# Decoding weights with an integer addition, and the last score tile of a head in one pass

## The chip, the cores and the metric

The kernel runs on one core of one Trainium2 chip. The metric is the device time of one execution in microseconds (us), lower is better. TensorE (PE) runs matmuls and loads its stationary operand (PEld), VectorE (DVE), ScalarE (ACT) and GpSimd (POOL) work elementwise, and SyncE (SP) issues most DMAs. Each engine takes its instructions in the program's order.

## The reference

Attention with a threshold over 4 batches of 8 heads (576 positions, head width 64), then two feed-forward blocks on 2304 tokens of width 512:

```python
scores = scale * np.matmul(q, k.transpose(0, 1, 3, 2))
thresh = np.max(scores, axis=-1, keepdims=True) - tau
scores = np.where(scores >= thresh, scores, -1000000000.0)
attn = exp(scores - max); attn = attn / (sum + 1e-09); x = attn @ v
...
h = x @ w_in                                     # 512 -> 2048
g = np.where(h >= 1, h, np.where(h <= -1, 0.0, (h + 1) ** 2 / 4)); y = g @ w_out
...
h = y @ w_in2; solu = h * softmax(h)             # 512 -> 1024
out = (layernorm(solu) * g_ln) @ w_out2
```

The four weight matrices come as 64-bit floats (the launch hands them over as 64-bit integers); the kernel turns them into 32-bit floats on the chip.

## The kernel before

**Precision.** A 32-bit product is made of matmuls on fp32r tiles: an operand is split into a rounded part (hi) and a rest (lo), and three products are summed.

**Attention** comes first (about 0 to 361 us). The 32 heads go in 16 pairs, a pair in 9 units: 4 units for the even head, one for the rests of 64 keys of both heads, 4 for the odd head. Each unit makes scores turned around (tile zt, keys on partitions), subtracts the row's threshold within the matmuls, and then: ACT takes the exponential (e, L416), DVE masks it (L421), ACT rounds it (phi, L429), POOL makes the rest (plo, L430), and three units later (LAGV) PE multiplies with the values (av, `values`, L453).

Ahead of that a head needs its row maxima: five score tiles (`scores`, L319) of 128 queries, the last with 64 queries and 64 empty rows, each of two passes of two matmuls with 288 columns. Stacked operands make a pass: q_st holds lo of q in its upper 64 rows and hi in its lower ones, k_st hi above and lo below, so pass one sums the two mixed products; q_m and k_on give hi times hi in pass two. `row_max` (L335) reduces a tile from PSUM on DVE; `row_shift` follows on ACT and POOL. Scores of a pair are made in units -10 to -2 relative to its own first one (S_UNITS), so the even head's tiles begin in the ninth unit of the second pair before it and end in the fourth unit of the pair before, and the odd head's begin in the fifth unit of that pair, two there.

**Stacking.** A head's q and k are transposed on PE (tr, L271), split on ACT and DVE (q_st L279, lo L280), and moved into place by DMAs that SP issues: `stack_k` (k_both<-q_st, k_both<-lo, q_m<-q_st, L289 to L291) and two units later `stack_q` (q_st<-lo, L295), which must wait until k_both<-q_st has landed, since it overwrites what that one reads. On the same queue stand the stores of finished heads (sums<-xs, x<-xs, L467 and L468, behind ACT's copy xs<-av, L465), loads of later pairs, and the weight loads raw (L542, 512 KB each).

**Buffers.** Score tiles, zt tiles and transposes take turns in three PSUM buffers (ps_r); a tile can start when the reader of the third one before it is through.

**Order.** Within a unit a string of letters (ORDER) sets the order: E zt and exponential, S a score tile, x its maximum, M the mask, p phi and plo, v and V values, J a step of the decode jobs, F, P, A, T, L the rest. A job is a Python generator; after each yield it waits so many steps, and in some units (DECODE) only certain kinds of step are let in: kind "b" in attention only in a pair's fourth unit. In attention 8 blocks of weights (128 by 512) are decoded one after the other, a new one at least 14 units after the last and at most two under way; 40 more follow later, up to three under way and a new one every third step.

**Decoding** (`words_to_f32`, L506): on the 32-bit halves of the numbers, ACT takes the absolute value of the upper half, DVE clamps, shifts and combines (L514, L517, L520), cuts out the power of two (L524) and scales the lower half with it (L527), POOL adds it (L531); ACT and POOL then split into hi and lo (L558, L560).

**First feed-forward block** (to about 757 us): per 128 columns of h, 12 matmuls (L793), then DVE, ACT, DVE, ACT and POOL make g (cl, gh, gl, L811 to L816), then 12 matmuls for y (L833). **Second block** to the end (L877, L988).

Of the kernel before, what the change touches and what calls it, by code (L numbers as in the profile page):

```python
# [21 lines left out]
def kernel(  # L22
# [16 lines left out]
    P = 128  # L39
# [26 lines left out]
    KEEP = {-8: 1, -7: 1, -6: 1, -5: 1, -4: 1, -3: 4, -1: 6, 0: 4, 1: 4, 2: 4}  # L66
    TURN_AT = 4
    JOB_EVERY = 14

# [90 lines left out]
    q_m = bufs4([R3, SP], F32R, "q_m")  # L160
    NV = 10
    v_nat = [early_p.tile([P, NV, D], F32, name=f"v_nat{i}") for i in range(2)]
    v_hi = [att_p.tile([P, NV, P], F32R, name=f"v_hi{i}") for i in range(2)]
    v_lo = [att_p.tile([P, NV, D], F32R, name=f"v_lo{i}") for i in range(2)]
# [16 lines left out]
    def setup_fill(i, eng):  # L181

        for j in range(2):
# [15 lines left out]
    def setup_ones():  # L199
        for t in v_hi:  # L200
            nc.gpsimd.memset(f32(t[:, 0:8, D:P]), 1.0)
            for half in range(2):
                for n in range(2):
                    nc.gpsimd.memset(f32(t[64 * half : 64 * half + 64, 8 + n, D:P]), float(n == half))

# [79 lines left out]
    def stack_k(h):  # L285
# [4 lines left out]
        nc.sync.dma_start(f32(k_st[j][i][D:P, o]), f32(tr_t[h][0:D, :]))  # L290
        nc.sync.dma_start(f32(q_m[j][i][0:D, 0:S]), f32(q_st[j][i][D:P, 0:S]))  # L291

    def stack_q(h):
# [22 lines left out]
    sc_ps = {}  # L316
    mcol = {}

    def scores(h, n):  # L319
        j, i = buf(h)  # L320
        o = key_off(h)
        ps = ps_r.tile([P, 2, 512], F32, tag="r", name="sc")
        for st, kk in ((q_st, k_st), (q_m, k_on)):
            r = slice(0, P if st is q_st else R1)
            for c in range(2):
# [4 lines left out]
                    start=(st is q_st),  # L330
                    stop=(st is q_m),
                )
        sc_ps[h, n] = ps

    def row_max(h, n):  # L335
        if n == 0:
            mcol[h] = att_p.tile([P, NTI], F32, tag="mcol", name="mcol", bufs=2)
        mc = mcol[h]
# [96 lines left out]
    def values(u, j):  # L435
# [14 lines left out]
        vh, vl = v_hi[p % 2][:, vn, :], v_lo[p % 2][:, vn, :]  # L450
        for o, vv, pp in ((P, vh, hi), (D, vl, hi), (P, vh, lo)):
            for c in range(2):
                nc.tensor.matmul(  # L453
                    ps[0:o, c, 0:HS], lhsT=vv, rhs=pp[:, c, :],
                    start=first and pp is hi and o == P, stop=last and pp is lo,
                )
            yield

    def store_head(h):
# [3 lines left out]
        else:  # L463
            xs = raw_p.tile([P, 1024], F32, tag="raw", name="xs")[:, 0:S].rearrange("p (c s) -> p c s", c=2)
        nc.scalar.copy(xs, av_ps.pop(h)[:, :, 0:HS])  # L465
        r = slice(D * (hh % 2), D * (hh % 2) + D)
# [39 lines left out]
    def words_to_f32(raw, n, got):  # L506

        upper, lower = raw[:, :, 1], raw[:, :, 0]
        a = wt_p.tile([P, 512], F32, tag="w", name="dec_a")[:, 0:n]
        au, cu = a.bitcast(U32), upper  # L510
        c = cu.bitcast(F32)
        nc.scalar.activation(out=a, in_=upper.bitcast(F32), func=ACTF.Abs)
        yield 1, "s"
        nc.vector.tensor_scalar(a, a, MAG_LOW, MAG_HIGH, op0=ALU.max, op1=ALU.min)  # L514
        if fine[0]:
            yield 1, "s"
        nc.vector.tensor_scalar(au, au, 3, 0x3FFFFFF8, op0=ALU.logical_shift_left, op1=ALU.bitwise_and)  # L517
        if fine[0]:
            yield 1, "b"
        nc.vector.scalar_tensor_tensor(  # L520
            out=au, in0=upper, scalar=0xC0000000, in1=au, op0=ALU.bitwise_and, op1=ALU.bitwise_or
        )
        yield 1, "s"
# [181 lines left out]
    for p in range(NP):  # L705
        s_units = S_FIRST[p] if p < 2 else S_UNITS
        for n, d in enumerate(s_units):
            at(s_at, UNITS * p + d, None, 2 * p + n // NTI, n % NTI)
        for j in range(2):
# [9 lines left out]
    def attention_unit(u):  # L719
# [7 lines left out]
        sc = iter(s_at.get(u, ()))  # L727
        mx = iter(s_at.get(u, ()))
        for what in ORDER[u % UNITS]:
            if what == "E" and 0 <= u < NU:  # L730
# [9 lines left out]
            elif what == "x":  # L740
                for _, a in itertools.islice(mx, 1):
                    row_max(*a)
            elif what == "M" and 0 <= u < NU:
                mask(u)
            elif what == "p" and 0 <= u - 1 < NU:
# [425 lines left out]
```

## Time and profile before

| | us |
|---|---|
| median of 3 runs | 968.86 (968.29 to 971.03) |
| profiled execution | 968.04 |
| its span, first to last instruction | 966.3 |
| PE busy in it | 944.8 |
| DVE, ACT, POOL busy in it | 711.9, 493.9, 603.3 |

The profile is of one execution. Times in it count from the first instruction. A matmul's duration covers its way through the array, and matmuls overlap, so what one costs is the distance between starts. "Idle before" is the time in which the engine had nothing to do ahead of an instruction, and behind the arrow stands what ended it, as far as the trace can tell. The granted clock of PE is full over the whole span (mean 0.999 of 2.4 GHz).

### The profile page before, as it was taken

How to read it: one execution, taken by the hardware profiler on the slowest of the kernel's cores; microseconds unless marked ns; L12 is line 12 of the kernel's file. 1: busy time of each engine (PE TensorE's matmuls, PEld its weight loads, DVE VectorE, ACT ScalarE, POOL GpSimd, SP SyncE). 2: the span in 40 equal slices, each digit the busy share in tenths (PEclk: the TensorE clock that was granted, in tenths of full speed). 3: DMA queues.
4: the chain of work that ended last, by engine and by line, in shares of the span. 5: the costliest groups of instructions: out<-in, count | busy, mean ns of one | idle time of the engine just before them, and what ended most of it. 6: DMA issues, size and time to landing. Idle time of an engine off the chain costs nothing.

```text
span 966.3 us, 15184 instructions
## 1 busy us (share of the span) xinstructions
PE 944.8 (98%) x5299; PEld 842.3 (87%) x5299; DVE 711.9 (74%) x1132; ACT 493.9 (51%) x924; POOL 603.3 (62%) x575
## 2 busy tenths in 40 slices
PE   7999999999999989999999999999999999999998
PEld 7899899999989978889888988898889988888886
DVE  5788888788788875898678876888675676666562
ACT  3667677777767675354333433333334444344433
POOL 7678788888978898677445544654547614334422
PEclk9999999999999999999999999999999999999999
DMA  6665666657666314211311131112311124444443
GB/s 144 148 147 124 152 159 145 170 126 176 157 142 154 81 44 98 68 66 44 120 44 66 44 119 45 65 45 77 129 34 45 44 66 131 109 120 124 138 119 90
DMA packets 89726, 99.61 MB, mean 103 GB/s; under 512 B 50000, under 2 KB 62608, under 8 KB 89648
## 3 DMA queue, kind: packets, MB, share of 16 engines
q1 hardware_dynamic: 87952, 97.97, 38.5%
q8 instruction: 42, 0.69, 0.3%
q10 hardware_dynamic: 1696, 0.66, 0.3%
q14 instruction: 36, 0.29, 0.1%
HBM read 55.13 MB, written 15.88 MB: 73 GB/s over the span
## 4 chain that ended last, share of the span: by engine, by line
PE 79%; POOL 8%; issue 4%; DVE 4%; ACT 3%; DMA 1%; ACTq 0%; POOLq 0%; DVEq 0%
PE y L833 18%; PE h L793 18%; PE o L988 10%; PE h L877 10%; PE av L453 9%; PE zt L403 6%; PE sc L326 6%; POOL plo L430 3%; PE tr L271 1%; POOL wg L560 1%; DMA nat<-in_q_dram 1%; DVE mcol L339 1%; POOL dec_a L531 1%; POOL xl L769 1%; ACT phi L429 1%
## 5 line engine op out<-in xcount | busy, mean ns | idle before, releaser
L430 POOL TENSOR_TENSOR plo<-e,phi 128x576 fp32r<-128x576 f32 x144 | 207.6, 1451 | 48.9 <-ACT phi L429 48.8
L816 POOL TENSOR_TENSOR gl<-cl,gh 128x512 fp32r<-128x512 f32 (+1 forms) x80 | 100.3, 1254 | 160.0 <-ACT gh L815 85.3
L793 PE MATMUL h<-xh,wg 128*128 128x512 f32 (+1 forms) x640 | 184.1, 369 | 0.7 <-DVE e L421 0.7
L833 PE MATMUL y<-gh,wg 128*128 128x512 f32 (+1 forms) x640 | 184.6, 369 | 0.0
L421 DVE SCALAR_TENSOR_TENSOR e<-zt,ntau,e 128x576 f32<-128x576 f32 x144 | 117.3, 815 | 54.5 <-ACT e L416 34.8
L793 PEld LDWEIGHTS h<-xh,wg 128*128 128x128 f32 x640 | 118.4, 188 | 16.7 <-DVE e L421 1.0
L833 PEld LDWEIGHTS y<-gh,wg 128*128 128x128 f32 x640 | 118.5, 188 | 15.9
L416 ACT ACTIVATE e<-zt 128x576 f32<-128x576 f32 x144 | 93.9, 652 | 70.0 <-PE zt L403 53.2
L339 DVE TENSOR_REDUCE mcol<-sc 128x1 f32<-128x576 f32 x160 | 116.7, 748 | 4.9 <-PE sc L326 4.7
L833 PE MATMUL y<-gl,wg 128*128 128x512 f32 (+1 forms) x320 | 118.8, 371 | 0.9 <-POOL gl L816 0.9
L793 PE MATMUL h<-xl,wg 128*128 128x512 f32 (+1 forms) x320 | 117.8, 368 | 0.0
L815 ACT CAST gh<-cl 128x512 fp32r<-128x512 f32 (+1 forms) x80 | 46.3, 579 | 111.9 <-DVE cl L814 110.7
L812 ACT ACTIVATE cl<-cl,half 128x512 f32<-128x512 f32 (+1 forms) x80 | 54.4, 679 | 95.4 <-DVE cl L811 95.4
L988 PE MATMUL o<-wg,ln 128*128 128x512 f32 x432 | 102.7, 393 | 0.0
L877 PE MATMUL h<-wg,y 128*128 128x512 f32 x432 | 101.1, 390 | 0.0
L988 PEld LDWEIGHTS o<-wg,ln 128*128 128x128 f32 x432 | 80.9, 188 | 18.8 <-ACT ln L951 0.4
L429 ACT CAST phi<-e 128x576 fp32r<-128x576 f32 x144 | 96.2, 668 | 1.5 <-ACT mt L369 0.7
L952 POOL TENSOR_TENSOR ln<-land,ln 128x1024 fp32r<-128x1024 f32 x16 | 38.5, 2404 | 91.7 <-ACT ln L951 85.0
L877 PEld LDWEIGHTS h<-wg,y 128*128 128x128 f32 x432 | 81.0, 188 | 16.8
L811 DVE TENSOR_SCALAR cl<-h 128x512 f32<-128x512 f32 (+1 forms) x80 | 50.6, 632 | 51.1 <-PE h L793 49.0
L326 PE MATMUL sc<-k_both,q_st 128*128 128x288 f32 x320 | 72.2, 307 | 6.5 <-issue 1.8
L403 PE MATMUL zt<-q_st,k_both 128*128 128x288 f32 x320 | 72.4, 308 | 1.6 <-DVE lo L280 1.3
(114 smaller groups left out, 1883.2 us busy)
## 6 DMA issues: line engine op xcount, KB each, us to landing
raw<-in_moe_w_in_dram SPq DMA_DIRECT2D x24, 512.0 KB
raw<-in_moe_w_out_dram SPq DMA_DIRECT2D x24, 512.0 KB
k_both<-q_st SPq DMA_DIRECT2D x30, 288.0 KB
sq<-so SPq DMA_DIRECT2D x64, 128.0 KB
land<-sq SPq DMA_DIRECT2D x16, 512.0 KB
k_both<-lo SPq DMA_DIRECT2D x32, 144.0 KB
q_st<-lo SPq DMA_DIRECT2D x32, 144.0 KB
x<-xs SPq DMA_DIRECT2D x32, 144.0 KB
```

Of the source, the lines that this page charges most:

```text
L326: nc.tensor.matmul(ps[:, c, 0:HS], lhsT=st[j][i][r, n * P : n * P + P], rhs=kk[j][i][r, o + c * HS : o + (c + 1) * HS], start=(st is q_st) ...
L339: nc.vector.tensor_reduce(mc[:, n : n + 1], sc_ps.pop((h, n))[:, :, 0:HS], axis=AXES.XY, op=ALU.max, negate=True)
L403: nc.tensor.matmul(ps[:, c, 0:HS], lhsT=st, rhs=mv[:, c * HS : (c + 1) * HS], start=(m == 0), stop=(m == len(todo) - 1),)
L416: nc.scalar.activation(out=e, in_=st_ps[u][:, :, 0:HS], func=ACTF.Exp)
L421: nc.vector.scalar_tensor_tensor(out=e, in0=st_ps.pop(u)[:, :, 0:HS], scalar=ntau[:, 0:1], in1=e, op0=ALU.is_ge, op1=ALU.mult)
L429: nc.scalar.copy(hi, e)
L430: (nc.vector if u - NU in LO_DVE or u < NU - UNITS and u % UNITS in LO_UNITS else nc.gpsimd).tensor_tensor(lo, e, f32(hi), op=ALU.subtract)
L793: nc.tensor.matmul(ps, lhsT=a[:, kk, f], rhs=m[:, kk, :], start=(n == 0 and kk == 0), stop=(n == 2 and kk == KD - 1),)
L816: nc.gpsimd.tensor_tensor(gl, cl, f32(gh), op=ALU.subtract)
L833: nc.tensor.matmul(y_ps[c][d], lhsT=a[:, jj, ds_], rhs=m, start=(jj == 0 and n == 0), stop=(jj == JG - 1 and n == 2),)
L877: nc.tensor.matmul(ps[g], lhsT=a[:, kk, :], rhs=wg_t["in2", g][s][:, kk, :], start=(n < 2), stop=(n >= 6 * KD - 2),)
L988: nc.tensor.matmul(ps, lhsT=a[:, f, :], rhs=wg_t["out2", f // 4][m][:, f % 4, :], start=(n == 0), stop=(n == len(terms) - 1))
```

## The change

Three edits.

*Decoding.* The shift keeps no mask, the sign is put in by exclusive or, and the two DVE steps L524 and L527 are gone. ACT instead turns the lower half into a float 2 + lower * 2^-51, whose bit pattern is a constant plus the rounded top bits of the lower half, and POOL adds the two patterns as 32-bit integers. In attention a job has two yields fewer, later one.

*One pass.* For heads from the third pair on, the last score tile takes only pass one: a further DMA (q_st<-q_st) puts hi of the 64 queries into the 64 empty columns, so that the matmul gives the mixed products on partitions 0 to 63 and hi times hi on 64 to 127. ACT copies the second half down (main), DVE adds and reduces in one instruction, which stands behind the mask of the unit. Odd heads make this tile first of five instead of last.

*Narrower.* v_hi carries 2 columns of ones instead of 64, so that the stationary operand of two of three av groups has 66 columns instead of 128, and only 65 partitions of av are copied. The tiles mcol become two fixed ones, zeroed at the start.

```diff
     def stack_k(h):
         ...
         nc.sync.dma_start(f32(q_m[j][i][0:D, 0:S]), f32(q_st[j][i][D:P, 0:S]))
+        if h >= ONE_PASS:
+            nc.sync.dma_start(f32(q_st[j][i][0:D, S:SP]), f32(q_st[j][i][D:P, M4:S]))
...
     def scores(h, n):
-        for st, kk in ((q_st, k_st), (q_m, k_on)):
+        passes = ((q_st, k_st), (q_m, k_on))[0 : 2 if n < NM or h < ONE_PASS else 1]
+        for st, kk in passes:
...
     def row_max(h, n):
+        mc = mcol[h] = mcols[h % 2]
+        if n == NM and h >= ONE_PASS:
+            ps = sc_ps.pop((h, n))
+            t = att_p.tile([64, 2, HS], F32, tag="half", name="main", bufs=1)
+            nc.scalar.copy(t, ps[64:P, :, 0:HS])
+            def finish():
+                nc.vector.tensor_tensor_reduce(
+                    out=t, in0=ps[0:64, :, 0:HS], in1=t, scale=-1.0, scalar=3.0e38,
+                    op0=ALU.add, op1=ALU.min, accum_out=mc[0:64, n : n + 1],
+                )
+            return finish
...
     def values(u, j):
-        for o, vv, pp in ((P, vh, hi), (D, vl, hi), (P, vh, lo)):
+        for o, vv, pp in ((VW, vh, hi), (D, vl, hi), (VW, vh, lo)):
...
     def words_to_f32(raw, n, got):
-        nc.vector.tensor_scalar(au, au, 3, 0x3FFFFFF8, op0=ALU.logical_shift_left, op1=ALU.bitwise_and)
+        nc.vector.tensor_scalar(au, au, 3, None, op0=ALU.logical_shift_left)
+        nc.scalar.activation(out=lower.bitcast(F32), in_=lower, func=ACTF.Copy, bias=2.0, scale=2.0 ** -51)
         if fine[0]:
             yield 1, "b"
         nc.vector.scalar_tensor_tensor(
-            out=au, in0=upper, scalar=0xC0000000, in1=au, op0=ALU.bitwise_and, op1=ALU.bitwise_or
-        )
-        yield 1, "s"
-        nc.vector.tensor_scalar(cu, au, 0xFF800000, None, op0=ALU.bitwise_and)
-        if fine[0]:
-            yield 1, "b"
-        nc.vector.scalar_tensor_tensor(
-            out=c, in0=lower, scalar=2.0 ** -52, in1=c, op0=ALU.mult, op1=ALU.mult
+            out=au, in0=upper, scalar=0x80000000, in1=au, op0=ALU.bitwise_and, op1=ALU.bitwise_xor
         )
         yield 1, ""
-        nc.gpsimd.tensor_tensor(a, a, c, op=ALU.add)
+        nc.gpsimd.tensor_tensor(au, au, lower, op=ALU.add)
...
+            m = n % NTI
+            if p > 1 and n >= NTI:
+                m = (m + NTI - 1) % NTI
```

How it moves instructions, first on PE in the fourth and fifth unit of the ninth pair, before and after (numbers tell buffers: 98 and 103 are of the even head 18, 102 and 107 of the odd head 19, whose scores begin here; `sc` score tile, `zt` turned scores, `av` values):

```order
L403 MATMUL zt<-q_st_105,k_both_100 128x288 x2
L403 MATMUL zt<-q_m_110,k_both_100 128x288 x2
L326 MATMUL sc<-k_both_98,q_st_103 128x288 x2
L326 MATMUL sc<-k_both_98,q_m_108 128x288 x2
L453 MATMUL av<-phi,v_hi_115 128x288 x2
...
L403 MATMUL zt<-q_m_111,k_both_101 128x288 x2
L326 MATMUL sc<-k_both_102,q_st_107 128x288 x2
L326 MATMUL sc<-k_both_102,q_m_112 128x288 x2
L326 MATMUL sc<-k_both_102,q_st_107 128x288 x2
L326 MATMUL sc<-k_both_102,q_m_112 128x288 x2
```

```order
L421 MATMUL zt<-q_st_105,k_both_100 128x288 x2
L421 MATMUL zt<-q_m_110,k_both_100 128x288 x2
L334 MATMUL sc<-k_both_98,q_st_103 128x288 x2
L471 MATMUL av<-phi,v_hi_115 66x288 x2
...
L421 MATMUL zt<-q_m_111,k_both_101 128x288 x2
L334 MATMUL sc<-k_both_102,q_st_107 128x288 x4
L334 MATMUL sc<-k_both_102,q_m_112 128x288 x2
```

The even head's last tile and the odd head's first have lost their second pass; nothing else stands between them than before.

On DVE in the same two units, before and after (`raw` and `dec_a` are of decoding, `mcol` are row maxima, `ISA` is the joint add and reduction with the reading of its accumulator):

```order
L280 SCALAR_TENSOR_TENSOR lo<-tr,scale_119,q_st_104 128x576
L339 TENSOR_REDUCE mcol<-sc 128x1
L421 SCALAR_TENSOR_TENSOR e<-zt,ntau,e 128x576
L527 SCALAR_TENSOR_TENSOR raw<-raw 128x512
L421 SCALAR_TENSOR_TENSOR e<-zt,ntau,e 128x576
L339 TENSOR_REDUCE mcol<-sc 128x1 x2
```

```order
L284 SCALAR_TENSOR_TENSOR lo<-tr,scale_119,q_st_104 128x576
L439 SCALAR_TENSOR_TENSOR e<-zt,ntau,e 128x576
L351 ISA main,mcol_122<-sc,main 64x576
L351 ISA mcol_122 64x1
L439 SCALAR_TENSOR_TENSOR e<-zt,ntau,e 128x576
L351 ISA main,mcol_123<-sc,main 64x576
L351 ISA mcol_123 64x1
L357 TENSOR_REDUCE mcol_123<-sc 128x1
```

The reduction of the even head's last tile moved behind the mask, and the decode step between the two masks is gone here; in 8 of the 14 pairs concerned a decode step stands before the second mask, where before it was all 14.

On SP around a weight load, before ahead of an odd head's stacking, and after within an even head's (`raw` the load, `k_both` and `q_st` the stacking):

```order
L468 DMA x<-xs 64x576
L542 DMA raw<-in_moe_w_out_dram 128x1024
L289 DMA k_both_101<-q_st_106 64x2x576
L290 DMA k_both_101<-lo 64x576
L291 DMA q_m_111<-q_st_106 64x576
```

```order
L293 DMA k_both_100<-q_st_105 64x2x576
L294 DMA k_both_100<-lo 64x576
L295 DMA q_m_110<-q_st_105 64x576
L297 DMA q_st_105<-q_st_105 64x64
L553 DMA raw<-in_moe_w_out_dram 128x1024
L301 DMA q_st_105<-lo 64x576
```

Of the loads in attention that have a head's stacking close behind, five stood ahead of an odd head's k_both; after, two do, two stand between an even head's k_both and its q_st<-lo, and one between an odd head's.

## Rows read from the trace of the kernel before

**Rows 1.** Page, busy time of each engine, share of the span, instructions.

```profile
PE 944.8 (98%) x5299; PEld 842.3 (87%) x5299; DVE 711.9 (74%) x1132; ACT 493.9 (51%) x924; POOL 603.3 (62%) x575
```

**Rows 2.** Windows: stretch, us, busy us of engines (count), clock, DMA.

```profile
100.00:200.00 100.00, 97.29 (x713) 93.44 (x712) 82.18 (x113) 72.40 (x140) 83.29 (x86) 1.00 0.64 154
400.00:450.00 50.00, 49.12 (x240) 42.93 (x240) 44.56 (x57) 23.23 (x42) 37.54 (x29) 1.00 0.24 80
```

**Rows 3.** Timeline, PE: start, us, what, count; three av groups.

```profile
202.35 0.43 PE L453 MATMUL av<-phi,v_hi 128*128 128x288 f32 x2
202.62 0.42 PE L453 MATMUL av<-phi,v_lo 128*64 128x288 f32 x2
202.88 0.43 PE L453 MATMUL av<-plo,v_hi 128*128 128x288 f32 x2
```

**Rows 4.** Page, costliest groups: count, busy us, mean ns, idle before, its end.

```profile
L833 PE MATMUL y<-gl,wg 128*128 128x512 f32 (+1 forms) x320 | 118.8, 371 | 0.9 <-POOL gl L816 0.9
...
L326 PE MATMUL sc<-k_both,q_st 128*128 128x288 f32 x320 | 72.2, 307 | 6.5 <-issue 1.8 <-DVE dec_a L520 1.6 <-DMA q_st<-lo 1.4
```

**Rows 5.** Timeline, SP and PE, to an odd head's first score tile.

```profile
201.66 0.55 SPq L295 DMA_DIRECT2D q_st<-lo  x1
...
203.95 0.43 PE L403 MATMUL zt<-q_m,k_both 67*128 67x288 f32 x2
...
204.21 0.49 PE L326 MATMUL sc<-k_both,q_st 128*128 128x288 f32 x2
```

**Rows 6.** Timeline, PE and SP: the same tile in two other pairs.

```profile
268.55 0.50 PE L326 MATMUL sc<-k_both,q_st 128*128 128x288 f32 x2 [1.64 <-DVE dec_a L520]
...
328.34 0.59 SPq L295 DMA_DIRECT2D q_st<-lo  x1
...
330.88 0.51 PE L326 MATMUL sc<-k_both,q_st 128*128 128x288 f32 x2 [0.52 <-issue]
```

**Rows 7.** Timeline, DVE and PE, fifth unit of the pair of rows 5.

```profile
204.18 1.03 DVE L527 SCALAR_TENSOR_TENSOR raw<-raw 128x512 f32<-128x512 uint32 x1
...
205.16 0.82 DVE L421 SCALAR_TENSOR_TENSOR e<-zt,ntau,e 128x576 f32<-128x576 f32 x1
...
206.13 0.43 PE L403 MATMUL zt<-q_st,k_both 128*128 128x288 f32 x2
```

**Rows 8.** Groups by form, whole span, DVE, ACT and POOL.

```profile
L339 DVE TENSOR_REDUCE mcol<-sc 128x1 f32<-128x576 f32 x160 | 116.7, 748 | 4.9 <-PE sc L326 4.7 <-POOL q_st L190 0.2
...
L527 DVE SCALAR_TENSOR_TENSOR raw<-raw 128x512 f32<-128x512 uint32 x48 | 39.7, 826 | 1.4
...
L524 DVE TENSOR_SCALAR raw<-dec_a 128x512 uint32<-128x512 uint32 x48 | 27.5, 573 | 0.0
...
L905 DVE DVE_READ_ACCUMULATOR so<-h,st,so 128x1 f32 x36 | 3.0, 83 | 0.0
...
L465 ACT COPY xs<-av 128x576 f32<-128x576 f32 x32 | 20.5, 640 | 26.9 <-PE av L453 22.3 <-DMA nat<-in_k_dram 1.5 <-DMA k_both<-lo 1.5
...
L531 POOL TENSOR_TENSOR dec_a<-dec_a,raw 128x512 f32<-128x512 f32 x48 | 67.4, 1403 | 5.1 <-DVE raw L527 5.1
...
L952 POOL TENSOR_TENSOR ln<-land,ln 128x1024 fp32r<-128x1024 f32 x16 | 38.5, 2404 | 91.7 <-ACT ln L951 85.0 <-PE o L988 6.8
```

**Rows 9.** Groups by form, whole span, weight loads of av.

```profile
L453 PEld LDWEIGHTS av<-phi,v_hi 128*128 128x128 f32 x320 | 50.9, 189 | 2.9 <-ACT xs L465 1.7
...
L453 PEld LDWEIGHTS av<-phi,v_lo 128*64 128x64 f32 x320 | 42.3, 135 | 0.0
```

**Rows 10.** Timeline, DVE and PE, a shift at the third unit's end.

```profile
116.21 1.61 DVE L517 TENSOR_SCALAR dec_a<-dec_a 128x512 uint32<-128x512 uint32 x1
...
118.60 0.54 PE L403 MATMUL zt<-q_st,k_both 128*128 128x288 f32 x2 [0.68 <-DVE lo L280]
```

**Rows 11.** Timeline, POOL and PE near the end of attention.

```profile
341.99 1.29 POOL L560 TENSOR_TENSOR wg<-dec_a,wg 128x512 fp32r<-128x512 f32 x1
...
344.71 0.53 PE L453 MATMUL av<-plo,v_hi 128*128 128x288 f32 x2 [0.84 <-POOL plo L430]
```

More of the change, by code (lines that the diff above doesn't have):

```diff
@@ L67 @@
     TURN_AT = 4
+    ONE_PASS = 4
     JOB_EVERY = 14
@@ L161 @@
     NV = 10
+    VW = D + 2
     v_nat = [early_p.tile([P, NV, D], F32, name=f"v_nat{i}") for i in range(2)]
-    v_hi = [att_p.tile([P, NV, P], F32R, name=f"v_hi{i}") for i in range(2)]
+    v_hi = [att_p.tile([P, NV, VW], F32R, name=f"v_hi{i}") for i in range(2)]
     v_lo = [att_p.tile([P, NV, D], F32R, name=f"v_lo{i}") for i in range(2)]
@@ L181, in setup_fill @@
     def setup_fill(i, eng):
+        if i < 2:
+            eng.memset(mcols[i], 0.0)
         for j in range(2):
@@ L200, in setup_ones @@
         for t in v_hi:
-            nc.gpsimd.memset(f32(t[:, 0:8, D:P]), 1.0)
+            nc.gpsimd.memset(f32(t[:, 0:8, D:VW]), 1.0)
             for half in range(2):
                 for n in range(2):
-                    nc.gpsimd.memset(f32(t[64 * half : 64 * half + 64, 8 + n, D:P]), float(n == half))
+                    nc.gpsimd.memset(f32(t[64 * half : 64 * half + 64, 8 + n, D:VW]), float(n == half))
     nat_t = {}
@@ L317 @@
     mcol = {}
+    mcols = [att_p.tile([P, NTI], F32, name=f"mcol{i}") for i in range(2)]
     def scores(h, n):
@@ L330, in scores @@
                     start=(st is q_st),
-                    stop=(st is q_m),
+                    stop=(st is passes[-1][0]),
                 )
@@ L335, in row_max @@
     def row_max(h, n):
-        if n == 0:
-            mcol[h] = att_p.tile([P, NTI], F32, tag="mcol", name="mcol", bufs=2)
-        mc = mcol[h]
+        mc = mcol[h] = mcols[h % 2]
[9 more added lines that the diff above has]
+            return finish
         nc.vector.tensor_reduce(
@@ L454, in values @@
                     ps[0:o, c, 0:HS], lhsT=vv, rhs=pp[:, c, :],
-                    start=first and pp is hi and o == P, stop=last and pp is lo,
+                    start=first and pp is hi and o == VW, stop=last and pp is lo,
                 )
@@ L464, in store_head @@
             xs = raw_p.tile([P, 1024], F32, tag="raw", name="xs")[:, 0:S].rearrange("p (c s) -> p c s", c=2)
-        nc.scalar.copy(xs, av_ps.pop(h)[:, :, 0:HS])
+        nc.scalar.copy(xs[0:R1], av_ps.pop(h)[0:R1, :, 0:HS])
         r = slice(D * (hh % 2), D * (hh % 2) + D)
@@ L509, in words_to_f32 @@
         a = wt_p.tile([P, 512], F32, tag="w", name="dec_a")[:, 0:n]
-        au, cu = a.bitcast(U32), upper
-        c = cu.bitcast(F32)
+        au = a.bitcast(U32)
         nc.scalar.activation(out=a, in_=upper.bitcast(F32), func=ACTF.Abs)
@@ L707 @@
         for n, d in enumerate(s_units):
-            at(s_at, UNITS * p + d, None, 2 * p + n // NTI, n % NTI)
+            m = n % NTI
+            if p > 1 and n >= NTI:
+                m = (m + NTI - 1) % NTI
+            at(s_at, UNITS * p + d, None, 2 * p + n // NTI, m)
         for j in range(2):
@@ L728, in attention_unit, with run_behind @@
         mx = iter(s_at.get(u, ()))
+        masked, behind = False, []
+        def run_behind():
+            while behind:
+                f = behind.pop(0)
+                if f:
+                    f()
         for what in ORDER[u % UNITS]:
@@ L741, in attention_unit @@
                 for _, a in itertools.islice(mx, 1):
-                    row_max(*a)
-            elif what == "M" and 0 <= u < NU:
-                mask(u)
+                    behind.append(row_max(*a))
+                if masked:
+                    run_behind()
+            elif what == "M":
+                if 0 <= u < NU:
+                    mask(u)
+                masked = True
+                run_behind()
             elif what == "p" and 0 <= u - 1 < NU:
```

## Prediction

> **What bounds the kernel now.** I read the busy line first. TensorE (PE) is busy 98% of the span, so the question is only which removed work stood on PE's own path and which waits PE still has [rows 1]. The windows then split the span [rows 2]. In the attention stage (100 to 200 us) PE is busy 97.29 of 100 us, while DVE has 82.18 and POOL 83.29. In the second stage (400 to 450 us) PE has 49.12 of 50. From 450 us on PE has no idle time that a lighter DVE could give back: the chain of waits there is one matmul row after another.
>
> "Busy" hides how long a matmul really takes, because matmuls overlap. So I read starts: three groups of two matmuls with 288 columns start at 202.35, 202.62 and 202.88 [rows 3]. That is 0.265 us a group, 0.133 us a matmul, whichever operand is loaded.
>
> The idle time that PE does show in front of score tiles is 6.5 us in all, 1.4 of it behind DMAs of q_st<-lo at the start [rows 4].
>
> **One pass instead of two, 28 heads.** Two matmuls fall away per head: 28 x 0.265 = 7.4 us of PE work, half of it in the even heads' tile and half in the odd heads'. What of it reaches the end is decided by what PE meets next.
>
> *Even heads' tile.* It stands in the fourth unit of a pair, between the copy of a finished head out of PSUM and the first score tile of the next odd head. That first tile needs q_st<-lo, a DMA that SP issues only behind the store of the finished head. In the pair shown the DMA is issued at 201.66 and the tile starts at 204.21, 2.55 us later, with PE unbroken before it: its last group began at 203.95, 0.26 us earlier [rows 5]. Was that luck or a limit? In the last pair, where PE comes early, the same tile waits visibly (0.52 us idle) and starts at 330.88, 2.54 us after the issue at 328.34 [rows 6]. So 2.54 us is what the transfer needs, and in the pair shown PE arrives at the very moment of its landing. If the even tile gives PE 0.265 us between the two, PE waits that long. I take 0 us; the other end is all 14 x 0.265 = 3.7 us.
>
> *Odd heads' tile.* It is now that first tile, so its two matmuls are saved behind the wait. But DVE is close behind: a decode step of 1.03 us stands between two masks, the second mask runs from 205.16 for 0.82 us to 205.98, and the zt group that needs the mask's buffer starts at 206.13 [rows 7]. So little is left there. Before, such a step stands in that unit of every pair (two steps of each decode are let in there alone); by the new order one of the two is gone, and 8 of 14 pairs keep one. There the new reduction, placed between the masks, makes DVE 0.15 us later, too. The 6 others keep 0.27 us each, 1.6 us; for the 8 I take half, 8 x 0.13 = 1.1 us. Sum **2.7 us**, bounds 0 and 3.7 us.
>
> *What it adds.* On ACT a copy, priced by xs<-av at 0.640 us, 28 times; ACT has a quarter of this stage free, and the copy runs while DVE masks. On DVE tensor_tensor_reduce is not in the trace: like the mask it reads PSUM and SBUF (0.82 us [rows 7]) and then reads its accumulator (0.083 us), against 0.748 us for the reduction it replaces, so +0.15 us [rows 8]; this is counted above. Behind the copy on ACT waits phi of the unit before, and on POOL plo, which PE needs only three units later; cover enough, and if not, 28 times up to 0.6 us. On SP one DMA more per head, some 0.55 us like q_st<-lo [rows 5]. In the odd heads it stands before the store of the finished head, whose data SP waits for anyway, in the even heads before a q_st<-lo that waits for the landing of k_both, so 0; without that cover it would be 0.55 us twice a pair. The wait of q_st<-q_st itself lands before q_st<-lo, which is issued later.
>
> **Narrower stationary operand** (66 columns for 128): loads of 128 columns take 0.189 us, of 64 columns 0.135 us [rows 9], but matmuls behind either start at the same distance, 0.27 and 0.26 us [rows 3]. I take 0 us, at most 640 x 0.005 = 3 us. The Trainium skill (TensorE: Matmul & The Clock Gate, "Step-by-step: what each phase is for") says that a load's time goes by its column count, which the load rows bear out, while the starts show that loads lie beside matmuls; were loads the bound, the sum would be the fourth rival's.
>
> **Decoding.** Per block DVE loses two steps, 0.573 and 0.826 us; ACT gets one, and POOL adds integers instead of floats [rows 8]. Where PE never waits (from 450 us on) that is worth 0. Four places are left.
>
> *Place of the steps in attention.* Two yields fewer move everything after them. A shift at the end of a pair's third unit delays lo behind it: 1.61 us of shift, then PE idle 0.68 us [rows 10]. By the new order such a shift stands there in four pairs, before in two: **-1.3 us** (bounds 0 and -1.4).
>
> *Weight loads in SP's queue.* Before, five of the 512 KB loads stand right ahead of an odd head's k_both, on whose landing q_st<-lo waits. The worst of them left PE idle 1.64 us [rows 6]; the other four cost less. By the new order two stand there, but two others stand between an even head's k_both and its q_st<-lo, and one between an odd head's. I take **0.2 us**; all idle before score tiles after the start, 6.5 - 1.4 = 5.1 us [rows 4], is the bound above, minus 3 us the one below.
>
> *End of attention.* The eighth block's decode ran into the last units, and the seventh's wg<-dec_a,wg took POOL 1.29 us at 341.99, after which PE stood 0.84 us for plo [rows 11]. By the new order all eight are over 27 units before the end. **1.0 us** (0 to 2).
>
> *Second stage.* PE waits 0.9 us for gl [rows 4], both times after decode steps that held DVE in front of cl. **0.9 us** (0 to 0.9). For POOL's integer add I take the float add's 1.403 us; L952's 2.404 us (twice the columns) is the bound above, and 1.0 us, a third less, the one below [rows 8].
>
> Everything else, the memsets and the copy of 65 partitions instead of 128, I put at 0: the first are off PE's path by several us, the second goes by columns.
>
> **The sum.** 2.7 - 1.3 + 0.2 + 1.0 + 0.9 = 3.5 us. The profiled execution took 968.04 us (span 966.3), so 964.5; the median of the runs is 0.8 us higher, so **965.3 us**.
>
> **Rivals.** (1) *All of PE's work comes back.* If the landing moves forward with PE, since the store ahead of it is itself PE's output, and DVE has room once its steps are fewer, 7.4 stands for 2.7: 8.2 us, 960.7 us. For it: PE is the busiest engine in every window. Against it: 2.54 against 2.55 us. (2) *Nothing comes back in the pairs.* Landing, mask and plo replace the missing matmuls one for one: 0 - 1.3 + 0.2 + 1.0 + 0.9 = 0.8, 968.1 us. For it: three limits within 0.15 us of each other. (3) *Slower: POOL's integer add.* If it costs 2.40 us, 1.0 more, each of the 8 in attention, and as many at the start of the second stage, delays what PE waits for. The 1.29 us at 341.99 cost PE 0.84, a share of 0.65, so 16 x 0.65 = 10.4 us, and 975.7 us. It cancels the gain from 0.34 us extra a piece on, and is visible as slower from 0.6 us (an add of 2.0 us). Against it: POOL's rows go by element count and not by operation. (4) *The weight loads are the bound.* PEld is busy 93.44 of 100 us in attention [rows 2]; 640 loads x 0.054 us = 35 us, 930 us. The Trainium skill (Trainium Kernel Development and Optimization, "Performance Expectations") wants closeness to the roof judged by the share of loads rather than of matmuls, and would read the stage so. Against it: the equal starts of rows 3.
>
> **How the numbers follow.** Forecast 0.46, rivals 0.24, 0.20, 0.07 and 0.03. A measurement can tell 0.3%, 2.9 us, from no change, so faster means below 965.9. The forecast's own range is 962.5 to 968.5 and six tenths of it lie below that: 0.28 + 0.24 + 0.03 = 0.55 faster. Slower is 0.07 and 0.02 from plo delayed by ACT's copy: 0.09. Same is 0.36. The range reaches to rival 1 with some more relief at the loads (958.5) and past rival 2 (969.5); rivals 3 and 4 stay outside.
>
> **What would show it.** Right: PE 0.27 us shorter per pair only behind the first odd tile, that tile still 2.54 us after its DMA and now with idle time ahead of it; no decode after 330 us; no wait for gl. The add's mean at POOL decides rival 3, the start distance of av groups rival 4. If the first odd tile shows no idle time, and pairs are 0.5 us shorter, my step on the landing was wrong. If pairs with a decode step in the fourth unit are as short as those without, the step on DVE was.

## The result and the profile after

The changed kernel takes **973.8 us** (median of 9 runs, 972.0 to 976.2) against 968.7 us (9 runs, 967.0 to 972.8) for the kernel before: a ratio of 1.0056, with an interval of 1.0043 to 1.007. It is slower by some 5 us. The forecast was 965.3 us, and the range ended at 969.5.

The profiled execution has a span of 973.6 us, before 966.3. First, where the 7.3 us lie. The first group of the last pair in attention, and the first group of the second stage (h), in the timeline of PE, before (L403, L793) and after (L421, L820):

```profile
341.32 0.43 PE L403 MATMUL zt<-q_st,k_both 128*128 128x288 f32 x2
...
360.71 0.74 PE L793 MATMUL h<-xh,wg 128*128 128x512 f32 x2 [0.75 <-DVE e L421]
```

```profile
352.42 0.43 PE L421 MATMUL zt<-q_st,k_both 128*128 128x288 f32 x2
...
369.99 0.73 PE L820 MATMUL h<-xh,wg 128*128 128x512 f32 x2 [0.80 <-DVE e L439]
```

The pairs up to the last lost 11.1 us. From the last pair to h the change gains 1.8 us (19.4 to 17.6), and behind it 2.0 us (605.5 to 603.6). So the loss is all in the steady pairs, and the two gains elsewhere are there, larger than forecast. Both are the decoding's: two_pass below, which keeps the new decoding and all matmuls, has 17.2 and 603.5 us there, old_decode 19.7 and 606.0. Of the second, 0.9 us is the wait for gl shown next; what the other 1.1 us are is not shown.

The page of after, next to [rows 1] and [rows 4] (busy time; costliest groups with idle time ahead), then the windows of [rows 2]:

```profile
PE 943.8 (97%) x5243; PEld 835.4 (86%) x5243; DVE 638.8 (66%) x1064; ACT 537.3 (55%) x1000; POOL 591.0 (61%) x577
...
L860 PE MATMUL y<-gl,wg 128*128 128x512 f32 (+1 forms) x320 | 118.4, 370 | 0.0
...
L421 PE MATMUL zt<-q_st,k_both 128*128 128x288 f32 x320 | 74.4, 314 | 8.9 <-DVE lo L284 4.3
L334 PE MATMUL sc<-k_both,q_st 128*128 128x288 f32 x320 | 70.2, 308 | 8.4 <-DVE e L439 2.3
```

```profile
100.00:200.00 100.00, 94.42 (x677) 87.77 (x676) 80.75 (x118) 79.29 (x154) 83.86 (x84) 1.00 0.64 152
400.00:450.00 50.00, 50.00 (x238) 43.27 (x237) 33.77 (x47) 26.62 (x49) 38.17 (x30) 1.00 0.23 76
```

In the second stage PE's last idle time has gone, and so has the wait for gl (0.9 us in [rows 4], 0.0 now). In attention PE is 94.42 of 100 us busy, 97.29 before [rows 2]: there are 56 matmuls fewer in the whole kernel, and more than their time stands empty. The new idle time is in front of zt, for lo and for the mask (e). Before, groups by form in the first 345 us had 1.6 us there:

```profile
L403 PE MATMUL zt<-q_st,k_both 128*128 128x288 f32 x304 | 68.9, 308 | 1.6 <-DVE lo L280 1.3 <-DVE e L421 0.2
```

**One such place.** The fourth and fifth unit of the tenth pair, after. Lines of ACT, DVE, POOL and PE from their timelines, put together by engine:

```profile
230.55 0.64 ACT L348 COPY main<-sc 64x576 f32<-64x576 f32 x1
231.09 0.68 ACT L447 CAST phi<-e 128x576 fp32r<-128x576 f32 x1
...
231.84 1.62 POOL L448 TENSOR_TENSOR plo<-e,phi 128x576 fp32r<-128x576 f32 x1 [0.99 <-ACT phi L447]
...
232.16 1.85 DVE L538 SCALAR_TENSOR_TENSOR dec_a<-raw,dec_a 128x512 uint32<-128x512 uint32 x1
233.94 0.80 DVE L439 SCALAR_TENSOR_TENSOR e<-zt,ntau,e 128x576 f32<-128x576 f32 x1
...
234.79 0.54 PE L421 MATMUL zt<-q_st,k_both 128*128 128x288 f32 x2 [0.79 <-DVE e L439]
```

Read it from the bottom. zt starts when the mask ends (233.94 + 0.80). The mask waits on DVE behind a decode step of 1.85 us. Such a step took 1.03 us in [rows 7]. Why 1.85? POOL's plo ends at 233.46, and the step at 234.01, 0.55 us later. In all eight decode steps of this line in attention the end is 0.55 us behind that of an instruction of POOL, whether the step lasts 1.17 or 1.86 us. In [rows 7] it was 0.55, too: the step ended at 205.21, and POOL's line there, from the timeline of before, ends at 204.66:

```profile
203.23 1.43 POOL L430 TENSOR_TENSOR plo<-e,phi 128x576 fp32r<-128x576 f32 x1 [0.34 <-ACT phi L429]
```

So DVE's step makes no headway while POOL works on SBUF, and then takes its 0.55 us. The Trainium skill (SBUF — State Buffer, "SBUF: two separate sides") says that a DVE instruction with two inputs in SBUF, as this one, and a GpSimd instruction that reads SBUF need the same port pair, an exclusive lock that the one who starts first holds for its whole instruction. The trace agrees as far as POOL comes first. And plo starts late here because ACT took the copy (main) ahead of phi.

**How time is counted below.** "Lost time" is, over the 13 pairs from the third to the fifteenth, the sum of the distances between starts of successive matmuls, less 0.133 us for 288 columns [rows 3] and 0.109 us for 128 (the distance within a head's transposes), by unit of the pair; a distance belongs to the unit of its later matmul. It is worked out from one profiled execution per kernel. The clock granted to TensorE also differs between executions of one kernel: 46 runs of the kernel before with a mean granted clock of 0.999 or more have a median of 967.7 us, the 16 with 0.996 or less one of 970.7. The third column is therefore the median of a kernel's runs at 0.999 or more, with their number.

| kernel | median us | at full clock (runs) | lost, units 1 to 4 | units 5 and 6 | units 7 to 9 | all |
|---|---|---|---|---|---|---|
| before | 968.7 | 967.7 (46) | 7.2 | 6.1 | 4.0 | 17.3 |
| after | 973.8 | 973.4 (6) | 8.6 | 20.5 | 5.8 | 34.9 |
| narrow_only | 968.9 | 967.7 (5) | 6.5 | 6.3 | 4.4 | 17.2 |
| two_pass | 970.3 | 968.3 (4) | 9.1 | 10.5 | 7.5 | 27.0 |
| old_decode | 975.8 | none | 6.9 | 18.8 | 3.6 | 29.3 |
| od_phi_first | 971.5 | 971.1 (2) | 7.1 | 12.9 | 6.9 | 26.9 |
| phi_first | 974.9 | 972.0 (1) | 8.3 | 16.2 | 10.3 | 34.8 |
| phi_first_t | 971.6 | 971.3 (4) | 10.4 | 10.9 | 11.9 | 33.1 |
| placed | 966.9 | 966.6 (6) | 10.3 | 9.3 | 7.0 | 26.7 |
| placed_early | 966.6 | 966.5 (6) | 10.6 | 8.2 | 6.8 | 25.7 |
| placed_two_pass | 963.7 | 963.7 (4) | 10.3 | 4.8 | 3.3 | 18.3 |
| placed_early_two_pass | 960.6 | 960.6 (3) | 10.6 | 1.0 | 3.4 | 15.0 |

After loses 17.6 us more than before and saves 13 x 0.53 = 6.9 us of matmuls. That is 10.7 us, nearly all of the 11.1 us above. In four profiles 1.7 us of the lost time is a stretch at a lower clock (last section): in units 5 and 6 of after and two_pass, in units 7 to 9 of phi_first and phi_first_t. The profiled execution of two_pass was also the longest of its ten (973.6 us).

### The profile page after: what moved, and what is told of

Read it like the earlier page. It is cut to its first block, busy times and chain, and to the rows that moved or that the text cites. A ratio compares the mean times of both kernels' runs of the same rounds, so it can differ in the third digit from the quotient of the medians.

```text
span 973.6 us, 15133 instructions
## 1 busy us (share of the span) xinstructions
PE 943.8 (97%) x5243; PEld 835.4 (86%) x5243; DVE 638.8 (66%) x1064; ACT 537.3 (55%) x1000; POOL 591.0 (61%) x577
## 4 chain that ended last, share of the span: by engine, by line
PE 75%; DVE 6%; POOL 5%; ACT 5%; DMA 3%; issue 3%; SPq 1%; ACTq 1%; DVEq 0%; POOLq 0%
PE y L860 20%; PE h L820 20%; PE o L1015 10%; PE h L904 10%; PE av L471 5%; PE zt L421 4%; PE sc L334 3%; POOL plo L448 3%; DVE e L439 2%; ACT phi L447 1%; DVE lo L284 1%; ACT e L434 1%; DVE mcol L357 1%; ACT xs L483 1%; ACTq L388 1%
## 5 line engine op out<-in xcount | busy, mean ns | idle before, releaser
L843 POOL TENSOR_TENSOR gl<-cl,gh 128x512 fp32r<-128x512 f32 (+1 forms) x80 | 97.4, 1217 | 162.6 <-ACT gh L842 107.1
L820 PE MATMUL h<-xh,wg 128*128 128x512 f32 (+1 forms) x640 | 184.0, 368 | 0.8 <-DVE e L439 0.8
L820 PEld LDWEIGHTS h<-xh,wg 128*128 128x128 f32 x640 | 118.4, 188 | 16.8 <-DVE e L439 1.1
L820 PE MATMUL h<-xl,wg 128*128 128x512 f32 (+1 forms) x320 | 117.8, 368 | 0.0
L357 DVE TENSOR_REDUCE mcol<-sc 128x1 f32<-128x576 f32 x132 | 96.9, 749 | 4.0 <-PE sc L334 3.8
L421 PE MATMUL zt<-q_st,k_both 128*128 128x288 f32 x320 | 74.4, 314 | 8.9 <-DVE lo L284 4.3
L334 PE MATMUL sc<-k_both,q_st 128*128 128x288 f32 x320 | 70.2, 308 | 8.4 <-DVE e L439 2.3
```

What stands on the lines that cost most here:

```text
L334: nc.tensor.matmul(ps[:, c, 0:HS], lhsT=st[j][i][r, n * P : n * P + P], rhs=kk[j][i][r, o + c * HS : o + (c + 1) * HS], start=(st is q_st) ...
L357: nc.vector.tensor_reduce(mc[:, n : n + 1], sc_ps.pop((h, n))[:, :, 0:HS], axis=AXES.XY, op=ALU.max, negate=True)
L421: nc.tensor.matmul(ps[:, c, 0:HS], lhsT=st, rhs=mv[:, c * HS : (c + 1) * HS], start=(m == 0), stop=(m == len(todo) - 1),)
L820: nc.tensor.matmul(ps, lhsT=a[:, kk, f], rhs=m[:, kk, :], start=(n == 0 and kk == 0), stop=(n == 2 and kk == KD - 1),)
L843: nc.gpsimd.tensor_tensor(gl, cl, f32(gh), op=ALU.subtract)
```

## The experiments

### Which part of the change

two_pass and narrow_only undo the tile (the first keeps the new decoding), old_decode undoes the decoding:

even_only keeps the tile on even heads (`h % 2 == 0` beside `h >= ONE_PASS` in `scores`, `row_max` and `stack_k`).

```diff
-    ONE_PASS = 4
+    ONE_PASS = 99                     (two_pass, narrow_only)
-            if p > 1 and n >= NTI:
+            if p > 99 and n >= NTI:   (these two, and even_only)
```

> The changed kernel with the last score tile of every head computed in two passes again and in the old order, with the old reduction and no copy on ACT; the new decoding and the 66-column operand stay. Theory A (the loss is the one-pass tile's: ACT's copy of half the tile stands ahead of phi and of the next exp, so the mask and zt come later): the loss goes, and the decoding's gain at the second stage shows, 966 us (965 to 968). Theory B (the loss is the decoding's: its steps fall into other units of a pair and hold DVE where PE waits for the mask): the loss stays, 973 to 976 us.

> The changed kernel with the decoding of before, all its steps and their places; the one-pass tile and the 66-column operand stay. Theory A: the loss of attention stays and the gain at the second stage goes, 974 to 978 us. Theory B: the loss goes and the matmuls saved show, 964 to 967 us.

> The kernel before with the 66-column operand alone (and the copy of 65 partitions that goes with it). Both theories: 968.7 us as before, within 1 us, av groups starting 0.13 us a matmul apart. A gain of 3 us or more would say that the weight loads do bound part of the stage.

> The changed kernel with the one-pass tile on even heads alone; odd heads have two passes, the old order and the old reduction. Theory A: the copy and the reduction are there 14 times instead of 28, so about half of the loss, 969 to 971 us. Theory B: as the changed kernel, 973 to 975 us.

Measured: two_pass 970.3 us (ratio 1.0012, 0.9994 to 1.0031), old_decode 975.8 (1.0068, 1.0045 to 1.0091), narrow_only 968.9 (1.0004, 0.9987 to 1.0021), even_only 972.5 (1.0038, 1.0026 to 1.005). The narrow operand is worth nothing, as forecast. By the medians the tile costs 6.9 us under the old decoding (975.8 - 968.9) and 3.5 us under the new (973.8 - 970.3), but the clocks of these runs differ. At full clock it is 5.1 us under the new (973.4 - 968.3). Old_decode has no such run, and its profile says 5.2 us (29.3 - 17.2 us lost, less 6.9 saved). So the tile costs some 5 us under either, and theory A holds for the place of the loss: it is the tile's. Even_only, with half of the tiles, lies between the two theories' ranges and decides nothing. The decoding did not give the 2 us that theory A had counted on: two_pass missed 966, at full clock too (968.3). It gained 4.2 us behind the pairs against narrow_only and lost somewhat more in them.

### ACT's copy ahead of phi

copy_only adds the copy alone to narrow_only, in `row_max`; od_phi_first and phi_first put phi first, in old_decode and in the changed kernel:

```diff
-        "FESvSSxxMxxpVLAPTJ",
+        "FESvSSpxxMxxVLAPTJ",
-        "FESSSMJvxxxpVLPAT",
+        "FESSSMpJvxxxVLPAT",
```

```diff
+        if n == NM and h >= 4 and h % 2 == 0:          (copy_only)
+            nc.scalar.copy(t, sc_ps[h, n][64:P, :, 0:HS])
-            yield 1, "s"                                 (phi_first_t, ahead of the shift)
+            yield 1, "t"
-    DECODE = ('', '', 's', 'asb', '', 's', '', 'as', 'as')
+    DECODE = ('', '', 's', 'asb', '', 's', '', 'ast', 'ast')
```

> The kernel before with the 66-column operand, and one thing added: in the even heads from the third pair on, ACT copies half of the last score tile to SBUF ahead of phi, as in the changed kernel, and nothing reads the copy. All matmuls, reductions and the decoding are as before. Theory A, made precise: the copy pushes phi back, so POOL's plo starts 0.6 us later and lies across the decode step on DVE in the fourth unit; that step goes from 1.03 to 1.85 us (it ends 0.55 us after plo), the mask behind it comes 0.8 us later and the next zt waits. 13 pairs by some 0.65 us, 977 us (975 to 980). Rival C (the copy is hidden, the loss comes from the PSUM buffer that the late reduction holds, from the added transfer or from the order of the odd heads' tiles): 969 us.

> The changed kernel with the decoding of before (as in old_decode, 975.8 us), and with phi ahead of the copy on ACT in the fourth and fifth unit of a pair. Theory A: plo starts as early as before the change, the decode step is back at 1.03 us, and the wait of zt is gone in 13 pairs: 967 us (965 to 969). Rival C: 974 to 977 us, since the reduction, the transfer and the order of the tiles stay.

> The changed kernel whole, with phi ahead of the copy on ACT in the fourth and fifth unit of a pair; PE and DVE keep their order. Theory A: the eight pairs with a decode step in the fourth unit are some 0.7 us shorter, 968 us (966 to 970). Rival C: 973 to 975 us.

> As phi_first, and the shift of the decoding is let in only at the end of a pair's eighth and ninth unit, so that no shift stands ahead of lo at the end of the third. Both theories on top of phi_first: the waits of zt for lo (4.2 us in all in the changed kernel) go, 3 to 4 us less than phi_first; theory A says 965 us (963 to 967), rival C 970 us.

Measured: copy_only 971.4 us (1.0029, 1.0008 to 1.005), od_phi_first 971.5 (1.0034, 1.0013 to 1.0054), phi_first 974.9 (1.0069, 1.0043 to 1.0095), phi_first_t 971.6 (1.0036, 1.0019 to 1.0054).

The mechanism is there in the rows, in the same unit of the same pair of phi_first:

```profile
229.06 0.67 ACT L447 CAST phi<-e 128x576 fp32r<-128x576 f32 x1
229.75 0.64 ACT L348 COPY main<-sc 64x576 f32<-64x576 f32 x1
...
229.80 1.42 POOL L448 TENSOR_TENSOR plo<-e,phi 128x576 fp32r<-128x576 f32 x1 [0.31 <-ACT phi L447]
...
231.10 0.68 DVE L538 SCALAR_TENSOR_TENSOR dec_a<-raw,dec_a 128x512 uint32<-128x512 uint32 x1
231.71 0.80 DVE L439 SCALAR_TENSOR_TENSOR e<-zt,ntau,e 128x576 f32<-128x576 f32 x1
...
232.66 0.44 PE L421 MATMUL zt<-q_st,k_both 128*128 128x288 f32 x2
```

plo ends at 231.22, the step takes 0.68 us, and zt no longer waits. Over all pairs that step's mean falls from 1.60 to 0.68 us (groups by form in the first 345 us, after, then phi_first):

```profile
L538 DVE SCALAR_TENSOR_TENSOR dec_a<-raw,dec_a 128x512 uint32<-128x512 uint32 x8 | 12.8, 1603 | 0.0
```

```profile
L538 DVE SCALAR_TENSOR_TENSOR dec_a<-raw,dec_a 128x512 uint32<-128x512 uint32 x8 | 5.4, 677 | 0.0
```

But the sizes were missed. With the old decoding, which has such a step in every pair, phi first gives back 4.3 us by the medians and 2.4 us in the profiled pairs (29.3 - 26.9); the second compares profiles without a low clock in the pairs. In the changed kernel it gives nothing that its four runs (972.0 to 976.6 us) can tell: 4.3 us less are lost in the fifth and sixth unit, and 4.5 us more in the seventh to ninth, 1.7 us of each the lower clock. And the copy alone costs 2.5 us, at full clock 3.7 (971.3 - 967.7), not 8: the reduction behind it waited for it, so the step began later, lasted 1.12 us on average, and the waits for late transfers in other pairs shrank. Mending one wait uncovers the next.

### Where the decoding's steps and loads stand

What did phi_first run into? In the same pair, SP's queue and PE:

```profile
233.90 0.58 SPq L553 DMA_DIRECT2D raw<-in_moe_w_out_dram  x1
234.53 1.10 SPq L510 DMA_DIRECT2D rb<-rec  x2
235.67 0.59 SPq L301 DMA_DIRECT2D q_st<-lo  x1
...
240.41 0.50 PE L334 MATMUL sc<-k_both,q_st 128*128 128x288 f32 x2 [1.45 <-DVE mcol L357]
```

A weight load of 512 KB stands ahead of q_st<-lo, and the tile starts 4.74 us behind that transfer's issue, where 2.54 us is usual [rows 6]. (The arrow names DVE's mcol, but that ended at 239.77.) The kernel placed is phi_first_t with loads let in only behind that transfer (kind "l", sixth and seventh item below), and placed_early issues an odd head's q_st<-lo ahead of the store:

```diff
-    DECODE = ('', '', 's', 'asb', '', 's', '', 'as', 'as')
+    DECODE = ('', '', 's', 'asb', '', 'sl', 'l', 'ast', 'ast')
-        "EvvSvSSMxxxVLFPATpJ",
+        "EvvSvSSMxxxVTLFPApJ",     (the early ones alone)
```

The new jobs may also start each pair (JOB_EVERY 9 for 14). The kernels called two_pass have no one-pass tile, no copy, and phi in its old place.

> The changed kernel with phi ahead of the copy (as phi_first), the shift at the end of a pair's eighth unit alone, and each 512 KB weight load issued right behind an even head's q_st<-lo instead of wherever the job before it ended. Theory D (what stayed in phi_first_t, 971.6 us, are late q_st<-lo: a weight load ahead of it in SP's queue makes its landing 4.6 instead of 2.4 us, and a score tile waits 1.3 to 1.7 us in the eighth unit): these waits go, 966 us (964 to 968). If the waits in the eighth unit have another cause, 971 us as before.

> As placed, and in a pair's third unit q_st<-lo of the odd head is issued before the store of the finished head, not behind it. Theory E (the step of the prediction: the landing 2.5 us after the issue holds the first odd tile and eats what the even head's tile saves): the tile starts with PE, each of 14 pairs is 0.1 to 0.2 us shorter, 964 us (962 to 966). If the mask alone sets that unit, the same time as placed.

> As placed, with the last tile of every head in two passes, the old order and the old reduction: the new decoding in better places alone. From two_pass (970.3 us) the waits for lo and in the eighth unit go: 965 us (963 to 967). Against placed it tells what the one-pass tile is worth once phi stands ahead of the copy: by theory A and E together nothing, 0 to 1 us, because the landing and the mask eat it.

> As placed_two_pass, with the early q_st<-lo. With two passes PE arrives at the landing, not before it, so theory E expects no more than 0.5 us from the early transfer here, 965 us, and 1 to 3 us between this kernel and placed_early, which is what the one-pass tile is then worth.

Measured: placed 966.9 us (0.9998, 0.998 to 1.0016), placed_early 966.6 (0.9985, 0.9972 to 0.9998), placed_two_pass 963.7 (0.9947, 0.9932 to 0.9962), placed_early_two_pass **960.6** (0.9936, 0.9914 to 0.9959). Theory D holds: the loads' places, with the new pace, are worth 4.7 us (971.6 to 966.9, and as much at full clock), and all places together 6.6 us without the tile (970.3 to 963.7), 4.6 at full clock. Theory E forecast the early transfer's worth the wrong way around: it gives 3.0 us with two passes and 0.3 us with one. The wait for the landing is there in both and goes in both: over the 13 pairs the first odd tile starts 4.4 us behind the pace of 0.133 us in placed and 0.2 us in placed_early, 4.0 us in placed_two_pass and nothing in placed_early_two_pass. With one pass something else takes its place. So the tile's price does not vanish when its first causes are mended; it is 3.2 us in placed and 6.0 us in placed_early. What eats it there? The second tile of the odd head (four matmuls of both tiles in one line), and DVE, in the ninth pair of placed_early:

```profile
203.22 0.64 ACT L348 COPY main<-sc 64x576 f32<-64x576 f32 x1
...
203.89 0.75 DVE L351 CUSTOM_DVE_ANT_0 main<-sc,main 64x576 f32<-64x576 f32 x1 [0.26 <-ACT main L348]
...
204.14 1.10 PE L334 MATMUL sc<-k_both,q_st 128*128 128x288 f32 x4
```

Four matmuls without a wait take 0.69 us (below); here they take 1.10, because the second pair of them needs the score buffer of the even head's last tile, and that one is held by the joint reduction until 204.64. In 12 places of this profile PE's idle time, 1.8 us in all, was ended by that reduction. Such a reduction used to stand ahead of the mask; now it waits for ACT, which comes later still when phi is first.

### Even heads, odd heads, their order, and the early transfer alone

pe_even, pe_odd and pe_odd_last are placed_early with the tile on one head of each pair; narrow_early is narrow_only with the early transfer.

```diff
-        if h >= ONE_PASS:
+        if h >= ONE_PASS and h % 2 == 1:   (pe_odd, pe_odd_last; == 0 in pe_even)
-            if p > 1 and n >= NTI:
+            if p > 99 and n >= NTI:            (pe_odd_last, pe_even)
```

> placed_early (966.6 us) with the one-pass tile on even heads alone, odd heads in two passes, the old order and the old reduction. Theory F (the even heads' late reduction holds the score buffer): the 0.3 us before the second tile of the odd head stays and eats the 0.2 us saved in the unit before, 962 us (961 to 964) against 960.6 us with none. Theory G (the loss sits with the odd heads' copy and reduction): 958 us, faster than with none.

> placed_early with the one-pass tile on odd heads alone, as the first of their five; even heads in two passes. Theory F: the buffer is free in time, the odd heads save up to 0.27 us a pair where the mask lets PE, 958 us (956 to 960). Theory G: ACT's copy and the reduction of the odd heads delay phi, plo and row shift up to the eighth unit, 963 to 967 us.

> As pe_odd, with the odd heads' one-pass tile as the last of their five, the old order. If the order costs nothing by itself: the time of pe_odd within 1 us. If the first place is what sets off the waits of the eighth unit (theory G): 2 us or more below pe_odd.

> narrow_only (the decoding and the two passes of before, 968.9 us) with q_st<-lo of the odd head issued before the store of the finished head. Theory E: in the kernel before PE arrives at the landing, so only the late landings behind weight loads are gained (1.75 us in one pair, up to 1 us in two others), 966 us (965 to 968).

Measured: pe_even 962.9 us (0.9953, 0.9936 to 0.9969), pe_odd 966.0 (0.9988, 0.9974 to 1.0002), pe_odd_last 969.9 (1.0021, 1.0011 to 1.003), narrow_early 964.3 (0.9961, 0.9947 to 0.9975). Against 960.6 us with no such tile, the even heads' tile costs 2.3 us and the odd heads' 5.4 us. At full clock it is 1.3 us (one run) and 5.1 us. So F and G are both there, and G is the larger. Behind the odd head's copy ACT's row shift (sh) is late, and with it POOL's rest and the transpose of it on PE; the odd head's maxima are late as well (here DVE stands idle for 0.41 us ahead of the joint reduction, for the copy). The same places in pe_odd and in placed_early_two_pass (ninth pair; its fourth unit begins at 204.81 and 198.09):

```profile
207.97 0.69 PE L334 MATMUL sc<-k_both,q_st 128*128 128x288 f32 x4
...
209.47 0.64 ACT L348 COPY main<-sc 64x576 f32<-64x576 f32 x1
210.01 0.73 ACT L263 CAST v_hi<-v_nat 128x640 fp32r<-128x640 f32 x1
210.64 0.20 ACT L367 ACTIVATE sh<-mcol 128x5 f32<-128x5 f32 x1
...
213.99 0.42 PE L421 MATMUL zt<-q_m,k_both 67*128 67x288 f32 x2
214.55 0.28 PE L381 MATMUL zt<-ident,mr 128*10 128x128 f32 x1
```

```profile
203.26 0.21 ACT L367 ACTIVATE sh<-mcol 128x5 f32<-128x5 f32 x1
...
207.17 0.43 PE L421 MATMUL zt<-q_m,k_both 67*128 67x288 f32 x2
207.44 0.28 PE L381 MATMUL zt<-ident,mr 128*10 128x128 f32 x1
```

sh starts 5.83 us behind that beginning with the copy and 5.17 without, and the transpose stands 0.56 us behind the group ahead of it instead of 0.27. Not every microsecond of the 5.4 is followed in this way. The order was no part of the harm: with the tile last, pe_odd_last is 3.9 us slower than pe_odd, since the copy then stands ahead of a finished head's (xs), and the next head's av waits for its PSUM buffer (13 times, 3.1 us; there are other waits as well). Neither of the two expected outcomes came. narrow_early, one letter of the order moved in the kernel before (plus the operand that is worth nothing), is 4.6 us faster than narrow_only (968.9), at full clock 3.4 us, where I had expected 3 us from late landings. The first odd tile's delay behind PE's pace falls there from 4.6 to 1.4 us, so this expectation was right in its cause.

## Why the prediction was wrong

**The copy on ACT** (taken as 0, "cover enough, and if not, 28 times up to 0.6 us"): this step failed. I followed phi to plo and plo to PE, where there were three units of cover. I did not ask what else POOL's plo touches while it runs. Moved by 0.6 us, it lay across a DVE step that [rows 7] had shown at 1.03 us, and that step moved the mask that PE needs at once. The rows had the clue: 1.03 us there against 0.826 us for the mean of the same line [rows 8], and 1.61 us for a shift [rows 10] against 0.573 us for the mean of another step with one input and as many columns [rows 8]. Such spreads for work of one size say that something else sets the time. Copy_only prices the copy alone, on even heads, at 2.5 us (3.7 at full clock). The 0.6 us a time stood in the text and behind 0.02 of the chances, but in no bound of the range.

**The tile's gain** (2.7 us, bounds 0 and 3.7): no bound below zero was given for the tile, and its worth is some -5 us under either decoding, and -3.2 and -6.0 us where phi, loads and transfer were mended. The reasoning on each limit was partly right. The landing does hold the first odd tile, now with idle time ahead of it as foretold: its delay grew from 4.3 us in before to 6.6 in after over the 13 pairs, and the early transfer takes it away. But the tile adds a step on ACT between PE and DVE, so the reduction that frees a score buffer comes later, and this was in no term. These two together, phi's delay and the late reduction, are what the runs put in the place of the gain of 2.7 us; how the 5 us divide between them is not shown. The 0.15 us allowed for DVE's reduction was fair (0.740 and 0.075 us against 0.748 of [rows 8]).

**Decoding in the pairs** (a net loss of 1.1 us): right in sign, far too small. Two_pass is 0.6 us slower than narrow_only at full clock though it gained 4.2 us behind the pairs, so the pairs lost nearly 5 us, an estimate. The shifts and clamps at the third unit's end were put at 1.3 us; letting the shift in elsewhere alone gave 3.3 us by the medians (974.9 to 971.6), 1.7 us in the profiled pairs. An instance in after, where not a shift but a clamp is held by plo (251.79 to 253.21; it ends 0.29 us later):

```profile
251.89 1.61 DVE L531 TENSOR_SCALAR dec_a<-dec_a 128x512 f32<-128x512 f32 x1
253.42 0.81 DVE L284 SCALAR_TENSOR_TENSOR lo<-tr,scale,q_st 128x576 fp32r<-128x576 f32 x1
...
254.28 0.40 PE L421 MATMUL zt<-q_st,k_both 128*128 128x288 f32 x1 [0.93 <-DVE lo L284]
```

The weight loads were put at a gain of 0.2 us; placing them gave 4.7 us. The prediction counted that two loads now stand between an even head's k_both and its q_st<-lo, and weighed them much like the five ahead of odd heads. The wait of 1.45 us above, behind one such load, is at an even head.

**End of attention and second stage** (1.0 and 0.9 us): right. The first measures 1.8 us, the second 2.0 us, of which the wait that the prediction named is 0.9.

**Rivals.** POOL's integer add takes 1.334 us against 1.403 for the float add, so the third rival, the way to "slower" that I priced, is out. The av groups of 66 columns still start 0.26 us apart (233.04, 233.30 and 233.57 in the tenth pair), so the fourth is out, too. The first two let the tile gain 7.4 us or nothing; neither lets it lose. "Slower" had 0.09 of the chance, 0.02 of it for the cause that the runs showed.

## What to carry to other kernels

Before a step is put in front of another on an engine with idle time, follow what it delays through every engine, and ask what those instructions share with their neighbours, not only who waits for their result. An instruction that shows several durations for one size may be set by its neighbour, as here: find the neighbour in the timeline before using its mean. And before matmuls are taken out at the price of a new hop between engines, look at what holds the buffers: here, under the new decoding, moving one transfer and the decoding's steps with all matmuls kept gave 0.6% (960.6 us), and no version with the one-pass tile reached that; the nearest, with the tile on even heads alone, took 962.9.

## What the runs showed of the hardware

DVE's decode steps, which have all operands in SBUF, stand still under POOL's instructions: a two-input step of 512 columns ends 0.55 us after plo and a one-input step 0.28 us after it, wherever it started beside it, so it takes 0.42 us (one input) or 0.68 us (two) alone and up to 1.6 or 1.86 us beside plo. The joint reduction, which has one operand in PSUM, took 0.74 us on average.

Some of the lost time is clock. In after PE's longest wait in attention, 1.55 us at 76.6 us, was followed by a stretch at the lower of TensorE's two levels (1.2 and 2.4 GHz); windows of 4 us, granted clock third from the end:

```profile
72.00:76.00 4.00, 4.00 (x28) 3.42 (x27) 3.61 (x6) 3.46 (x6) 2.23 (x2) 1.00 0.34 76
76.00:80.00 4.00, 2.45 (x16) 2.19 (x15) 2.07 (x4) 2.72 (x6) 1.44 (x2) 0.89 0.52 131
80.00:84.00 4.00, 4.00 (x23) 3.93 (x22) 2.46 (x6) 2.14 (x5) 3.85 (x6) 0.68 0.77 172
84.00:88.00 4.00, 4.00 (x31) 3.78 (x30) 3.74 (x5) 2.55 (x6) 2.25 (x2) 1.00 0.48 109
```

A share of 0.11 and 0.32 of two windows is missing, 4 x 0.43 = 1.7 us; it is part of the lost time above. That the wait brings the lower clock is not shown. The stretches within the pairs of phi_first, phi_first_t and two_pass also stand behind waits, of 1.45 to 1.57 us, but the kernel before waits 1.64 us ahead of 268.55 [rows 6] and two_pass 2.06 us ahead of 239.24, and neither shows such a stretch there. So a time that two kernels differ by can hold some clock, and is read with the granted clock beside it.
